# Two more chunks gathered by TensorE in four column groups, with x@w_ch of late pairs between the rounds

**Chip, cores, metric.** One core of one Trainium2 chip. The metric is device time in microseconds (us), the median of several executions.

## The reference

Causal attention with a bias, then a spectral layer: along the sequence, the first 64 modes of a real FFT are multiplied by complex matrices, transformed back to `y`, and a channel product with a relu ends it.

```python
def _moe_ref(x, w_r, w_i, w_ch):          # x is the attention's output, 8 x 576 x 512
    X = np.fft.rfft(x, axis=1)
    Xr, Xi = np.real(X[:, :64]), np.imag(X[:, :64])
    Yr = np.einsum('bmd,mde->bme', Xr, w_r) - np.einsum('bmd,mde->bme', Xi, w_i)
    Yi = np.einsum('bmd,mde->bme', Xr, w_i) + np.einsum('bmd,mde->bme', Xi, w_r)
    ...
    y = np.fft.irfft(Y, n=S, axis=1)
    u = x + y
    return (u + np.maximum(u @ w_ch, 0.0)).astype(np.float32)
```

## The kernel before

The 64 modes come in eight chunks of eight (`c` = 0 to 7; chunk five is `c` = 4). For each chunk `modes` multiplies with the weights w_r and w_i, which stream in from DRAM all the time; VectorE adds the earlier partial sums (`y_sb`), and the result stands as 128 rows of (mode, re/im, batch). The inverse transform wants the rows of all chunks on partitions and the batch in the free dimension: that tile is `yv`, with y (`which` = 0) and v = y@w_ch (`which` = 1). There are two ways into it. A *spread* is a DMA of 128 KB. A *gather* does it on TensorE: matmuls that pick the columns of a few batches, one column group for each, followed by copies by ScalarE and VectorE. Chunks one to four are gathered, chunks five to eight are spread, the last two of them also used directly. Between these steps `work()` puts a *pair* of x@w_ch, the product of two blocks of x with w_ch: transposes, two casts on VectorE, eight matmuls, and a copy of the product out of PSUM, where TensorE's results land. *Granted clock* below is the share of its full clock that TensorE was given.

```python
    def modes(g, c, meanwhile=None):
        ...                                    # 16 matmuls, 4 for each quarter of the weights
            yb = spool.tile([P, DM], FP16, name="y_sb", tag="y")
            ...                                # VectorE: yb = ps + y_acc[:, c]
            if c >= NCK // 2:
                spread(c, 0, yb)
            return yb

    def spread(c, which, rows):
        nc.sync.dma_start(out=yv[16 * c : 16 * c + 16, :, which, :], in_=rows)

    def gather(c0, c1):
        n = 2 * MC * (c1 - c0)
        rows = slice(2 * MC * c0, 2 * MC * c1)
        ng = P // n
        for b0 in range(0, B, ng):
            vp = auxpool.tile([P, DM], FP32, name="v_ps", tag="aux")
            yp = auxpool.tile([P, DM], FP32, name="yg_ps", tag="aux")
            for which, ps in ((1, vp), (0, yp)):
                for dt in range(DT):
                    for g in range(ng):
                        ...                    # matmul into column group g
                for g in range(ng):
                    dst, src = yv[rows, b0 + g, which, :], ps[n * g : n * g + n, :]
                    if g % 2:
                        nc.vector.tensor_copy(out=dst, in_=src)
                    else:
                        nc.scalar.copy(out=dst, in_=src)

    def work():
        ...
        if order_z:
            i = order_z.pop(0)
            x_transposed(i)                    # transposes, two casts on VectorE
            ahead.append(i)
        if len(ahead) == 2 or not order_z:
            keep(ahead.pop(0))                 # product, then a copy of it

    TAKE = (3, 2, 2, 0, 2, 1)

    for c in range(NCK - 2):
        yb = modes(NG - 1, c)
        for x in range(TAKE[c] - 1):
            work()
        yt = y_transposed(yb, c)
        if TAKE[c]:
            work()
        if c >= NY:
            y_times_wch(c, yt)                 # 4 matmuls, a VectorE copy, a spread
        elif c == NY - 1:
            gather(0, NY)                      # four rounds, two column groups
    work()
    c = NCK - 2
    x_transposed(0)
    x_times_wch(0, False)
    yb6 = modes(NG - 1, c)
    ...                                        # chunks seven and eight, then 18 pairs of output
```

(The kept pairs of kind "e" are copied once by ScalarE and once, as a difference, by VectorE: that second copy, L495 of 1.23 us, plays a part below.)

The softmax here doesn't subtract the row's maximum and nothing guards it: scores larger than these inputs give would overflow.

## Time and profile before

| | before |
|---|---|
| median of 6 executions | 458.11 us (456.71 to 459.57) |
| span of the profiled one | 458.0 us (its time: 459.76) |
| start of the first gather | 377.39 us |
| chunk six's, seven's modes start | 400.04, 409.96 us |
| chunk eight's modes: first, last quarter | 415.18, 419.44 us |

The span ends with the output, some 38.56 us after the start of the last quarter's matmuls.

The timeline of TensorE around chunk six, whose lines the change rewrites (start, length, line, tiles, idle time before and what ended it):

```profile
400.04 1.12 PE L441 MATMUL yp<-w_sb,xs 128*32 128x512 bf16 x16
401.96 0.40 PE L625 MATMUL yt_ps<-ident16h,y_sb 128*128 128x128 f16 x4 [0.80 <-DVE y_sb L455]
...
409.96 1.12 PE L441 MATMUL yp<-w_sb,xs 128*32 128x512 bf16 x16
```

From chunk six's modes to chunk seven's it is 9.92 us, 8.55 of them TensorE work.

### The profile page before, as it was taken

The numbers are of one execution on the slowest core, as the hardware profiler recorded it, in microseconds if no ns is written. First come the engines' busy times: TensorE is split into PE (matmuls) and PEld (weight loads), VectorE is DVE, ScalarE is ACT, GpSimd is POOL, SyncE is SP. The second block draws the span as 40 slices with busy tenths as digits, with TensorE's granted clock in tenths as the row PEclk, the third lists the DMA queues.
The fourth block names the chain that finished last, engine by engine and source line by source line (L and its number), as shares of the span: only waits on it lengthen the run. The fifth ranks groups of instructions, "written<-read, shape, count | busy, mean of one in ns | idle before, by whom it ended". The sixth has DMA issues, their size and how long they took to land.

```text
span 458.0 us, 10354 instructions
## 1 busy us (share of the span) xinstructions
PE 349.1 (76%) x4241; PEld 220.4 (48%) x4241; DVE 236.5 (52%) x528; ACT 223.5 (49%) x390; POOL 182.6 (40%) x269
## 2 busy tenths in 40 slices
PE   0798997976563969946587788679977867989996
PEld 0465665654342646624354555456643335444432
DVE  6675765753332636724345435556556423552676
ACT  1475887464242745723444444456632222321895
POOL 6655554454344555434453444455422321200000
PEclk9997999997777979967768769899999875699999
DMA  9999999999999999999999999999999999993697
GB/s 172 199 202 203 201 201 203 203 204 204 204 205 201 200 186 202 204 205 204 202 201 204 204 204 203 204 202 202 206 205 208 206 206 206 210 215 77 228 308 303
DMA packets 108800, 94.01 MB, mean 205 GB/s; under 512 B 28417, under 2 KB 103937, under 8 KB 108753
## 3 DMA queue, kind: packets, MB, share of 16 engines
q0 software_dynamic: 98960, 81.81, 112.9%
q1 hardware_dynamic: 9792, 11.55, 8.1%
q8 instruction: 33, 0.54, 0.4%
q14 instruction: 15, 0.11, 0.1%
HBM read 164.56 MB, written 9.44 MB: 380 GB/s over the span
## 4 chain that ended last, share of the span: by engine, by line
DMA 53%; PE 32%; DVE 6%; issue 4%; POOL 3%; ACT 1%; DVEq 0%; POOLq 0%
DMA w_sb<-in_moe_w_i_dram 28%; DMA q<-in_q_dram 13%; DMA w_sb<-in_moe_w_r_dram 5%; PE sc_ps L365 4%; DMA x_all<-in_moe_w_i_dram 4%; PE av_ps L394 4%; PE yp L441 3%; PE sc_ps L359 3%; PE tr_ps L324 2%; DMA y_acc<-in_moe_w_r_dram 2%; PE z_ps L602 2%; DMA k<-in_k_dram 2%; PE z_ps L692 2%; PE ft_ps L418 2%; PE u_ps L711 2%
## 5 line engine op out<-in xcount | busy, mean ns | idle before, releaser
L373 ACT ACTIVATE p_sb<-sc_ps,cumt_sb 128x576 f16<-128x576 f32 (+1 forms) x256 | 142.1, 636 | 46.2 <-PE sc_ps L365 45.7
L217 POOL DMA_DIRECT2D w_sb<-in_moe_w_i_dram x60 | 45.0, 751 | 87.3 <-PE yp L441 48.5
L217 POOL DMA_DIRECT2D w_sb<-in_moe_w_r_dram x60 | 45.4, 757 | 63.4 <-DMA w_sb<-in_moe_w_r_dram 23.3
L217 POOL DMA_DIRECT2D v<-in_v_dram x72 | 50.7, 706 | 31.5 <-DMA v<-in_v_dram 10.5
L324 PE MATMUL tr_ps<-ident,q 64*64 64x64 bf16 x576 | 18.1, 215 | 52.9 <-DMA q<-in_q_dram 52.8
L359 PE MATMUL sc_ps<-negm,ident 128*128 128x256 bf16 x256 | 57.1, 310 | 0.2
L441 PE MATMUL yp<-w_sb,xs 128*32 128x512 bf16 x480 | 36.9, 412 | 16.2 <-DMA w_sb<-in_moe_w_i_dram 11.1
L327 DVE COPY qtA<-tr_ps 64x576 bf16<-64x576 bf16 x32 | 23.7, 741 | 49.4 <-PE tr_ps L324 49.4
L344 ACT ACTIVATE p<-sc_ps,cumt 128x64 f16<-128x64 f32 x32 | 10.1, 314 | 75.7 <-PE sc_ps L340 75.7
L365 PE MATMUL sc_ps<-qtB,ktB 128*128 128x512 bf16 (+2 forms) x192 | 45.2, 354 | 0.0
L394 PE MATMUL av_ps<-v,p_sb 128*128 128x65 f16 x1024 | 44.3, 197 | 0.0
L394 PEld LDWEIGHTS <-p_sb 128*128 128x128 f16 x1024 | 39.3, 100 | 4.8 <-issue 0.5
L327 DVE COPY ktA<-tr_ps 64x576 bf16<-64x576 bf16 x32 | 24.0, 749 | 33.2 <-PE tr_ps L324 33.2
L324 PEld LDWEIGHTS <-q 64*64 64x64 bf16 x576 | 14.2, 127 | 55.6 <-DMA q<-in_q_dram 54.4
L365 PE MATMUL sc_ps<-qtA,ktA 65*128 65x512 bf16 (+2 forms) x192 | 37.4, 305 | 0.6 <-DMA qtA<-ncum_sb 0.6
L399 DVE TENSOR_REDUCE den<-av_ps 128x5 f32<-128x10 f32 x64 | 10.8, 169 | 49.0 <-PE av_ps L394 49.0
L441 PEld LDWEIGHTS <-xs 128*32 128x32 bf16 x512 | 22.7, 170 | 25.7 <-issue 22.0
L404 DVE TENSOR_TENSOR x_all<-av_ps,rcp 128x320 f16<-128x320 f32 x64 | 31.4, 491 | 2.2
L365 PEld LDWEIGHTS <-ktB 128*128 128x128 bf16 x192 | 23.0, 120 | 15.8 <-issue 7.1
L327 ACT COPY ktB<-tr_ps 64x576 bf16<-64x576 bf16 x32 | 20.3, 635 | 20.0 <-DVE ktA L327 19.1
L602 PE MATMUL z_ps<-wch_sb,xs 128*128 128x512 f16 x96 | 27.4, 437 | 0.8 <-DVE xs L596 0.8
L324 PE MATMUL tr_ps<-ident,k 64*64 64x64 bf16 x576 | 17.0, 207 | 13.3 <-DVE qtB L327 8.6
(116 smaller groups left out, 534.3 us busy)
## 6 DMA issues: line engine op xcount, KB each, us to landing
w_sb<-in_moe_w_r_dram POOLq DMA_DIRECT2D x60, 512.0 KB, 12.0
w_sb<-in_moe_w_i_dram POOLq DMA_DIRECT2D x60, 512.0 KB, 11.9
q<-in_q_dram POOLq DMA_DIRECT2D x32, 144.0 KB, 10.0
k<-in_k_dram POOLq DMA_DIRECT2D x32, 144.0 KB, 10.1
v<-in_v_dram POOLq DMA_DIRECT2D x72, 64.0 KB, 9.7
out_dram<-r_sb SPq DMA_DIRECT2D x16, 256.0 KB, 2.1
out_dram<-r_w SPq DMA_DIRECT2D x16, 256.0 KB, 2.5
x_all<-in_moe_w_i_dram POOLq DMA_DIRECT2D x3, 512.0 KB, 10.1
```

Of the source, the lines that this page charges most:

```text
L217: nc.gpsimd.dma_start(out=dst, in_=src)
L324: nc.tensor.transpose(ps[rows, r, :], src[rows, r, :], ident16[rows, rows])
L327: copy(out=dst[n % NQ][rows, :].rearrange("d (p r) -> d p r", r=R), in_=ps[rows].rearrange("d r p -> d p r"),)
L344: nc.scalar.activation(out=p4[n % 2][:, :NL], in_=ps, func=ACTF.Exp, bias=cumt4[:, b * (H // 2) + g : b * (H // 2) + g + 1], scale=0.125,)
L359: nc.tensor.matmul(ps[:, bass.ds(w * S, W)], ident16, negm[:, bass.ts(r, W)], start=True, stop=False, skip_group_check=True,)
L365: nc.tensor.matmul(ps[:, c0 : c0 + i1 - i0], keys[:, w, r, :], qt[:, i0:i1], start=False, stop=True, skip_group_check=True,)
L373: nc.scalar.activation(out=pt[:, poff[x] : poff[x] + S - w * W], in_=ps[:, w * S : (w + 1) * S - w * W], func=ACTF.Exp, bias=cumt_sb[:, x, ...
L394: nc.tensor.matmul(ps[:, I, r : r + NCH], lhsT, rhs, start=(i == 0), stop=(i == len(todo) - 1), skip_group_check=True,)
L399: nc.vector.tensor_reduce(out=den, in_=ps[:, :, 0 : VW : NCH], axis=mybir.AxisListType.X, op=ALU.add)
L404: nc.vector.tensor_tensor(out=x_all[:, g, b, :, D * h : D * h + D], in0=ps[:, :, 1 : NCH], in1=rcp.unsqueeze(2).to_broadcast([P, NT, D]), ...
L441: nc.tensor.matmul(ps[32 * cg : 32 * cg + 32, :], cols[:, c0 : c0 + 32, c * MC + 2 * cg + par], wt[(g, c, ri, par)][:, cg, :], start=(x == ...
L602: nc.tensor.matmul(z[:, x, :], xts[i][:, x, dt, :], wch_sb[:, dt, :], start=(dt == 0), stop=(last and dt == DT - 1), skip_group_check=True,)
```

## The change

Its intent: eight transfers of 128 KB become four, and waits of the gather rounds are covered by the product of a late pair (two of the four rounds of the first gather, one of the two of the second). Chunks five and six go through `yt_first` and a second gather of two rounds; as that one has 32 columns for each batch, four batches fit side by side (`ng` = 4).

```diff
-            if c >= NCK // 2:
+            if c >= NCK - 2:
                 spread(c, 0, yb)
...
-        yt = yt_first[:, :, c, :] if c < NY else spool.tile(...)
+        yt = yt_first[:, :, c % NY, :] if c < NCK - 2 else spool.tile(...)
...
-    def gather(c0, c1):
+    def gather(c0, c1, turns):
...
                         nc.scalar.copy(out=dst, in_=src)
+            if turns:
+                turns -= 1
+                work()
...
-    TAKE = (3, 2, 2, 0, 2, 1)
+    TAKE = (3, 2, 2, 0, 1, 0)
...
-        if c >= NY:
-            y_times_wch(c, yt)
-        elif c == NY - 1:
-            gather(0, NY)
+        if c == NY - 1:
+            gather(0, NY, 2)
+        elif c == NCK - 3:
+            gather(NY, NCK - 2, 1)
```

More of the change, by code (lines that the diff above doesn't have):

```diff
@@ L625, in y_transposed @@
             nc.tensor.transpose(ps[:, dt, :], yb[:, bass.ts(dt, P)], ident16h)
-        yt = yt_first[:, :, c, :] if c < NY else spool.tile([P, DT, P], FP16, name="yt_sb", tag="yt")
+        yt = yt_first[:, :, c % NY, :] if c < NCK - 2 else spool.tile([P, DT, P], FP16, name="yt_sb", tag="yt")
         nc.scalar.copy(out=yt, in_=ps)
```

## The prediction

> **What bounds the kernel now.** I read the page's 40 slices first, then the chain of waits, then the timeline of the end, then the busy time in windows of 3.41 us.
>
> In the slices (11.45 us each) DMA stays at 9 until slice 36, and the granted TensorE clock falls to 5 and 6 in slices 34 and 35, just before:
>
> ```profile
> PEclk9997999997777979967768769899999875699999
> DMA  9999999999999999999999999999999999993697
> ```
>
> The chain of waits says what follows whom. Until 375 us it runs through weight transfers. From 377.39 us it holds TensorE lines only, almost without a break; no weight transfer is on it any more:
>
> ```profile
> 355.01 19.81 DMA w_sb<-in_moe_w_i_dram
> 377.39 2.00 PE v_ps L653 x8
> 380.78 2.00 PE v_ps L653 x8
> ...
> 387.53 2.00 PE v_ps L653 x8
> 390.91 1.97 PE yp L441 x16
> ...
> 400.11 1.08 PE yp L441 x13
> ```
>
> So the end is set by TensorE from 377.39 us on, and a transfer saved there saves nothing by itself. (Last weights: a transfer takes 2.55 us at 206 GB/s, eight are in flight, so I put the last landing near 415.5 us; its matmuls start at 419.44 us. That is 4 us of slack.)
>
> What a gather round costs is read from the timeline (start, length):
>
> ```profile
> 380.78 1.98 PE L653 MATMUL v_ps<-wch_sb,yt_first 128*64 128x512 f16 x8 [0.96 <-DVE yv L663]
> 382.80 0.58 ACT L665 CAST yv<-v_ps 64x512 f16<-64x512 f32 x1 [2.31 <-PE v_ps L653]
> 383.28 0.58 ACT L665 CAST yv<-yg_ps 64x512 f16<-64x512 f32 x1
> 383.41 0.69 DVE L663 CAST yv<-v_ps 64x512 f16<-64x512 f32 x1 [2.08 <-ACT yv L665]
> 384.02 0.69 DVE L663 CAST yv<-yg_ps 64x512 f16<-64x512 f32 x1
> 384.15 1.98 PE L653 MATMUL v_ps<-wch_sb,yt_first 128*64 128x512 f16 x8 [0.95 <-DVE yv L663]
> ```
>
> The reader should see two things. VectorE's copy out of a PSUM tile starts 0.03 us after ScalarE's copy out of the same tile ends (383.38): they take turns. And each of the four rounds makes the next user of that tile wait 0.95 us.
>
> The windows (length, PE busy, ..., granted clock, DMA share, GB/s) show what those gaps cost:
>
> ```profile
> 338.34:341.75 3.41, 1.90 (x28) 1.03 (x21) 2.10 (x5) 0.59 (x1) 2.20 (x3) 1.00 1.24 207
> 351.99:355.40 3.41, 1.36 (x17) 0.83 (x17) 1.80 (x3) 0.34 (x1) 1.13 (x2) 0.99 1.24 207
> 379.30:382.71 3.41, 2.45 (x23) 2.04 (x21) 1.30 (x2) 1.06 (x2) 0.74 (x1) 0.50 1.24 206
> 392.95:396.36 3.41, 3.41 (x15) 1.74 (x14) 1.85 (x3) 0.00 (x0) 1.92 (x3) 0.51 1.25 207
> ```
>
> A window with 1.36 us busy (40%) was followed by half clock, one with 1.90 us (56%) was not; at half clock 2.45 us (72%) did not bring the clock back, a full window did. From 375.9 to 396.4 us TensorE runs at half.
>
> **The Trainium skill.** "TensorE: Matmul & The Clock Gate", Part 1, What's actually happening: a free-running window of 3413 ns and two clock states. The trace agrees: the clock falls at 355.4, 365.6 and 375.9 us, three windows apart. Its Part 3 (packing small matmuls) says that matmuls in different column groups run side by side; here 16 of 128x32 take 1.06 us, where 16 full ones at 0.21 us would take 3.4. "PSUM — Partial Sum Buffer", PSUM bank collisions: two engines must not touch the same bank and quadrant at once, reads included; the turn-taking above is that guard, by tile. The same page, Engine vs sequencer instructions: VectorE's and ScalarE's queues are strict FIFO; no line of this trace contradicts it, and the argument below rests on it.
>
> **The change, part by part.** Chunks five and six lose their own product with w_ch (2 x 4 matmuls, 0.86 us each), two VectorE copies and four transfers of 128 KB. They gain a second gather of two rounds in four column groups. One pair's x@w_ch is put after each of the first two rounds of the old gather, and the last product (8 matmuls, no transposes) between the two new rounds. The order of instructions in the build confirms this, and its waits say that in the new rounds the copies of one tile go ScalarE, VectorE, ScalarE, VectorE, each waiting for the one before. Copies of 64x512 and of 128x512 take the same here (ScalarE 0.58 and 0.59 us, VectorE 0.69 both), so I keep 0.58 and 0.69 us for 32x512 (starts 0.48 and 0.61 apart on one engine). All clock times below are for the old run's window phase.
>
> *First gather.* Round one as before, at half clock, to 379.85. Then transposes (1.0) and products (8 x 0.427) follow with no wait. TensorE is busy for a whole window, so full clock comes near 382.7 instead of 396.4; the product ends near 383.5. Round two at full clock 0.89 + 0.45, transposes 0.61, products 1.73: 387.2. Round three 1.35; round four waits for copies (VectorE also has the pair's two casts and the pair's keep) until 389.7; it ends 391.1, and chunk five's modes wait until 392.2. One wait per round remains, 1.2 us each; 60% busy should hold the clock. Modes 1.12, the sum on VectorE 0.8 (now bare), transposes and one pair 2.4: chunk six's modes start at **396.6, against 400.04: 3.5 us gained**.
>
> *Second gather.* Modes 1.12, sum 0.8, transposes 0.4, copy 0.68: its first product starts near 399.55, and takes 1.06, so T0 = 400.6 is the end of the first product. After T0, in us:
> - Copies of v: ScalarE 0.25-0.83, VectorE 0.87-1.56, ScalarE 1.60-2.18, VectorE 2.22-2.91. Copies of y follow in the same alternation and end at 4.87.
> - TensorE: y part (estimated 0.8 from 16 small matmuls), product 1.73, done at 2.5; second v waits till 2.96, ends 4.02; second y waits for 4.9, ends 5.7.
> - ScalarE: the product's keep (1.01) after the copies, 4.04-5.05. Second-round copies from 4.96, eight in turn, last one ends at 9.58.
> - VectorE, in order: only then the two casts of pair 0, 9.50 and 10.11.
> - TensorE: transposes of pair 0 end at 6.15. Its product needs the first cast: 10.24. **Idle 4.1 us.** It ends at 12.0.
>
> Chunk seven's modes then start at 400.6 + 12.0 = 412.6, against 409.96. From chunk six's modes to chunk seven's it is 16.0 us instead of 9.9: 6.1 lost. Sum so far: +2.6 us.
>
> *Clock after the second gather.* An idle of 4.1 us leaves at least one window under 41% busy wherever the windows fall, so the clock halves. It returns only after a full busy window: 3 to 6 us at half, and as TensorE has no spare time there, half of that is lost: 1.4 to 3.1, I take 2.4.
>
> *The rest* (final modes, 18 pairs of output) is unchanged and TensorE-bound. Transfers: four spreads fewer, about 2.5 us less in the DMA queue at 206 GB/s, all inside the slack.
>
> Total: -3.5 + 6.1 + 2.4 = +5.0 us: **463.2 us**.
>
> **Rivals.**
> - *The first gather wins alone.* If the second gather's copies were hidden (say the product between its rounds covers them), only its matmuls cost: 2 x 1.86 - 1.72 = 2.0 us more, and -3.5 stands: about 456.7. For: the filling at the first gather does hide two waits. Against: eight alternating copies per round take 4.6 us after the product's end, and the filler lasts 1.7 us; nothing at all stands after the second round.
> - *No halving after the stall.* 460.8. For: 56% was once enough. Against: 4 us are longer than a window.
> - *The clock does not come back in the first gather*, because the windows fall badly or round three and four halve it again. Then the gain of 3.5 is nearly gone: 465 to 467.
> - *DMA limits the end after all.* The four spreads share the engines with the weights; then fewer transfers would gain up to 2 us. Against: 4 us of slack at the last modes.
>
> **Range and chances.** Free window phase moves both clock terms by some 1.5 us each; the stall is uncertain by 1 us (handovers, keep's place). So 460.0 to 466.0. Over 2% faster means under 449.0, for which no mechanism exists: 0.01. Over 2% slower means over 467.3: the stall plus bad clock in both places, 0.04.
>
> **What would show it.** Right: v copies of 32x512 of about 0.58 and 0.69 us alternating; TensorE idle some 4 us before the product of pair 0, released by VectorE's cast; clock 1.00 by about 383 us; then 0.50 in the stretch after the stall; chunk six's modes near 396.6, chunk seven's near 412.6; the output tail as long as before. Wrong: copies of one tile overlapping on the two engines, casts of pair 0 ahead of the copies, or a final-modes wait on a weight transfer.

## More of the kernel before

What TensorE waited for between 376 and 420 us is in the view of waits (engine, tile and line, what it waited for: us in total, times, longest):

```profile
PE v_ps L653 <- DVE yv L663: 2.9, 3, 1.0
...
PE yp L441 <- DVE yv L663: 1.0, 1, 1.0
PE z_ps L602 <- DVE xs L596: 0.8, 2, 0.6
```

The first two are the four waits of the gather for its copies, about 1 us each; the third says that a product with w_ch hardly ever waits for its casted transposes.

## The result

The kernel after takes 465.99 us in the median of 6 executions (464.29 to 467.01), against 458.11. The ratio is 1.0166, with a 95% interval of 1.0132 to 1.0199. (Ratios here are the mean time of one kernel's runs over that of the other's of the same rounds, so not quite the ratio of the medians quoted.) So it is slower by 1.7%, within the 2% that counts as the same. The profiled execution took 467.01 us, its span is 465.1. (Both profiled executions are slow ones of their kernel: the one before, with 459.76 us, lies above all six timed ones.)

The slices of the profile after, to set against those in the prediction:

```profile
PEclk9997999987586989957788799899998879979999
DMA  9999999999999999999999999999999999961697
```

A slice is now 11.63 us. The dip of the granted clock to 5 and 6 in slices 34 and 35 is gone, a shallower one (to 7) has come in slice 36. DMA falls to 6 in that slice and to 1 in the next; before it fell to 3 only in slice 37: now a stretch of little traffic lies between the last weights and the output.

The view of waits of the kernel after, TensorE, 376 to 426 us:

```profile
PE z_ps L602 <- DVE xs L596: 4.9, 2, 4.7
PE yt_ps L625 <- DVE y_sb L455: 3.8, 4, 1.9
PE v_ps L653 <- DVE yv L663: 1.6, 2, 1.0
...
PE yp L441 <- DVE yv L663: 1.0, 1, 1.0
PE yg_ps L653 <- DVE yv L663: 1.0, 1, 1.0
```

By the timeline the first gather's part of the last three is two waits of 1 us (ahead of round four and of chunk five's modes) instead of four, as intended; the second gather brings two of its own, 0.66 and 0.97 us. Above them stands one wait of 4.7 us of a product for VectorE's casts, and a wait of 1.9 us for the sum of chunk six. The timeline shows both in their place:

```profile
396.28 1.12 PE L441 MATMUL yp<-w_sb,xs 128*32 128x512 bf16 x16
397.44 1.23 DVE L495 TENSOR_TENSOR y_acc<-z_ps,y_acc 128x1024 f16<-128x1024 f32 x1 [1.71 <-ACT y_acc L494]
398.58 0.68 DVE L455 TENSOR_TENSOR y_sb<-yp,y_acc 128x512 f16<-128x512 f32 x1
399.32 0.40 PE L625 MATMUL yt_ps<-ident16h,y_sb 128*128 128x128 f16 x4 [1.92 <-DVE y_sb L455]
...
402.19 0.69 DVE L663 CAST yv<-v_ps 32x512 f16<-32x512 f32 x1 [2.93 <-ACT yv L665]
402.91 0.58 ACT L665 CAST yv<-v_ps 32x512 f16<-32x512 f32 x1 [0.75 <-DVE yv L663]
...
406.73 0.62 PE L592 MATMUL xt_ps<-ident16h,x_all 128*128 128x128 f16 x8
...
410.59 0.70 DVE L663 CAST yv<-yg_ps 32x512 f16<-32x512 f32 x1 [0.64 <-ACT yv L665]
411.32 1.29 DVE L596 CAST xs<-xt_ps 128x512 f16<-128x512 f32 x2
412.07 3.60 PE L602 MATMUL z_ps<-wch_sb,xs 128*128 128x512 f16 x8 [4.72 <-DVE xs L596]
415.59 1.38 PE L441 MATMUL yp<-w_sb,xs 128*32 128x512 bf16 x16
```

Read it from below. The product at 412.07 had waited 4.72 us for the casts at 411.32. The casts' input, the transposes of pair 0 at 406.73, had been ready since 407.35; but in VectorE's queue the casts stand behind its copies of the second gather, which take turns with ScalarE's copies of the same tile (the releasers in brackets). The product then took 3.60 us instead of 1.90, at half clock. The top four lines are the other wait: the sum of chunk six (L455) stood in VectorE's queue behind the second half of a kept product (L495), of 1.23 us.

The windows of the kernel after (stretch, length, busy time of PE, PEld, DVE, ACT, POOL, granted clock, DMA share, GB/s):

```profile
379.30:382.70 3.40, 3.40 (x21) 1.84 (x18) 2.59 (x4) 0.90 (x2) 0.74 (x1) 0.59 1.24 207
382.70:386.10 3.40, 3.40 (x32) 2.35 (x31) 1.90 (x3) 2.07 (x3) 0.74 (x1) 1.00 1.24 205
...
406.60:410.00 3.40, 0.75 (x23) 0.50 (x12) 2.07 (x3) 1.74 (x4) 0.00 (x0) 0.92 1.24 206
410.00:413.40 3.40, 1.33 (x4) 0.51 (x5) 1.99 (x3) 0.56 (x1) 0.00 (x0) 0.50 0.89 148
```

With a product behind round one the clock is full from some 382 us (before: 396.4). The stretch with the stall is 0.75 us busy, and half clock follows. The DMA share falls already in the last of these stretches, before chunk seven's modes begin: no weight is waited for.

**Where the 7.1 us of span went.** Offsets from the start of the first gather take out what happened ahead of it (the gather itself started at 377.39 before and 377.12 after, 0.3 earlier):

| stage | before | after | difference |
|---|---|---|---|
| start of gather to chunk six's modes | 22.65 | 19.16 | -3.49 |
| chunk six's to chunk seven's modes | 9.92 | 19.31 | +9.39 |
| to chunk eight's modes, first quarter | 5.22 | 5.48 | +0.26 |
| to its last quarter | 4.26 | 4.26 | 0 |
| to the end of the span | 38.56 | 39.77 | +1.21 |

Less the 0.27 of the earlier start it adds up to +7.10.

### The profile page after: what moved, and what is told of

It reads as the page before. It is cut to its first block, busy times and chain, and to the rows that moved or that the text cites. A ratio compares the mean times of both kernels' runs of the same rounds, so it can differ in the third digit from the quotient of the medians. Undisturbed runs are those within 1.5% of the kernel's fastest.

```text
span 465.1 us, 10436 instructions
## 1 busy us (share of the span) xinstructions
PE 343.0 (74%) x4265; PEld 219.7 (47%) x4297; DVE 241.2 (52%) x534; ACT 227.9 (49%) x398; POOL 182.7 (39%) x269
## 4 chain that ended last, share of the span: by engine, by line
DMA 61%; PE 24%; DVE 5%; issue 4%; POOL 3%; ACT 2%; DVEq 0%; POOLq 0%; ACTq 0%
DMA w_sb<-in_moe_w_i_dram 29%; DMA q<-in_q_dram 15%; DMA w_sb<-in_moe_w_r_dram 10%; PE yp L441 3%; PE z_ps L602 2%; PE sc_ps L365 2%; DMA k<-in_k_dram 2%; DMA y_acc<-in_moe_w_r_dram 2%; PE av_ps L394 2%; PE z_ps L695 2%; PE sc_ps L359 2%; PE tr_ps L324 2%; DMA y_acc<-in_moe_w_i_dram 2%; PE u_ps L714 2%; PE u_ps L695 2%
## 5 line engine op out<-in xcount | busy, mean ns | idle before, releaser
L359 PE MATMUL sc_ps<-negm,ident 128*128 128x256 bf16 x256 | 55.9, 304 | 0.2
L441 PE MATMUL yp<-w_sb,xs 128*32 128x512 bf16 x480 | 35.9, 405 | 17.3 <-DMA w_sb<-in_moe_w_i_dram 12.2
L365 PE MATMUL sc_ps<-qtB,ktB 128*128 128x64 bf16 (+2 forms) x160 | 34.8, 322 | 3.7 <-issue 2.0
```

Source lines behind the costliest of these rows:

```text
L359: nc.tensor.matmul(ps[:, bass.ds(w * S, W)], ident16, negm[:, bass.ts(r, W)], start=True, stop=False, skip_group_check=True,)
L365: nc.tensor.matmul(ps[:, c0 : c0 + i1 - i0], keys[:, w, r, :], qt[:, i0:i1], start=False, stop=True, skip_group_check=True,)
L441: nc.tensor.matmul(ps[32 * cg : 32 * cg + 32, :], cols[:, c0 : c0 + 32, c * MC + 2 * cg + par], wt[(g, c, ri, par)][:, cg, :], start=(x == ...
```

## The experiments

Twelve runs. Each timed one is compared with the kernel before on the same chip in the same rounds. "Theory" in the expectations is the prediction's: the first part (pairs between the rounds of the first gather) wins 3.5 us, the second part (the second gather) loses by alternating copies, by the place of the casts in VectorE's queue, and by the clock. The offsets below are those of the profiled executions, in us from the start of the first gather.

| run | time, us | ratio | 95% | chunk six's modes | seven's | eight's last quarter | rest of span |
|---|---|---|---|---|---|---|---|
| before | 458.11 | 1 | | 22.65 | 32.57 | 42.05 | 38.56 |
| after | 465.99 | 1.0166 | 1.0132-1.0199 | 19.16 | 38.47 | 48.21 | 39.77 |
| e1_first_only | 457.13 | 1.0002 | 0.9980-1.0023 | 20.37 | 29.82 | 40.52 | 38.51 |
| e1b_first_again | 456.90 | 0.9976 | 0.9962-0.9991 | 22.19 | 31.63 | 41.12 | 38.51 |
| e2_second_only | 468.12 | 1.0244 | 1.0224-1.0264 | 21.65 | 41.88 | 51.62 | 39.05 |
| e3_by_tile | 463.70 | 1.0151 | 1.0109-1.0193 | 19.42 | 36.05 | 45.51 | 39.58 |
| e4_pair0_early | 463.56 | 1.0121 | 1.0090-1.0152 | 21.34 | 35.82 | 46.15 | 39.95 |
| e5_stall_filled | 463.68 | 1.0124 | 1.0109-1.0139 | 19.11 | 36.72 | 46.20 | 38.85 |
| e6b_first_spread_twice | 466.18 | 1.0187 | 1.0172-1.0202 | 22.02 | 31.47 | 49.31 | 40.62 |
| e8_mended | 458.37 | 1.0008 | 0.9982-1.0033 | 19.34 | 33.63 | 43.09 | 39.00 |
| e9_mended_warm | 455.72 | 0.9960 | 0.9937-0.9983 | 18.46 | 30.13 | 39.62 | 38.80 |
| e10_spread_warm | 457.18 | 0.9989 | 0.9975-1.0003 | 19.83 | 28.43 | 41.45 | 38.58 |
| e11_first_no_spread | 457.19 | 0.9984 | 0.9965-1.0004 | 21.90 | 31.34 | 40.80 | 38.84 |
| e12_mended_best | 455.55 | 0.9948 | 0.9935-0.9961 | 16.69 | 27.94 | 39.60 | 38.81 |

### The two parts by themselves

**First part alone.** From the kernel before:

```diff
+    def gather(c0, c1, turns):          # and work() after a round while turns are left
-    TAKE = (3, 2, 2, 0, 2, 1)
+    TAKE = (3, 2, 2, 0, 1, 0)
-            gather(0, NY)
+            gather(0, NY, 2)
```

> The first gather of the change alone: two x@w_ch of pairs between its rounds; chunks five and six keep their own product and their four spreads. My theory (the second gather costs, the first gains): full clock from about 383 us, chunk six's modes near 397 instead of 400.0, chunk seven's near 406.5 instead of 410.0, time 454.5 us (ratio 0.992). Rival (the first gather's fill is worth nothing, the pairs only change places): 458.

Measured: 457.13 us, ratio 1.0002. The expected gain did not come. In the profiled execution (the fastest of the four) the clock was full and chunk six's modes came 2.3 us sooner, but chunk eight's then waited; this is the timeline of TensorE in e1_first_only:

```profile
413.89 0.45 PE L441 MATMUL yp<-w_sb,xs 128*32 128x512 bf16 x4 [1.10 <-DMA w_sb<-in_moe_w_i_dram]
```

So the last weights are a limit close behind TensorE. As one profile shows one execution, the kernel was run once more.

> The first gather of the change alone, once more, as the neighbour of the next run. Both theories: about 1.000 as in its first run; the last modes' weights land after TensorE is ready for them.

Measured: 456.90 us, 0.9976. This time no matmul of chunks seven and eight waited for weights; instead the clock fell, in the timeline and the windows of e1b_first_again:

```profile
390.02 1.96 PE L441 MATMUL yp<-w_sb,xs 128*32 128x512 bf16 x16 [0.98 <-DVE yv L663]
```
```profile
389.50:392.90 3.40, 2.08 (x18) 0.90 (x18) 1.77 (x3) 0.22 (x1) 1.71 (x3) 0.56 1.24 205
```

The modes of chunk five take 1.96 us where e1_first_only had 1.12: half clock from about 390 to 397 us, after rounds three and four, which have no pair behind them. The same kernel is thus held up by weights in one execution and by the clock in another, and wins 0 to 1 us.

**Second part alone.** From the kernel after:

```diff
-    TAKE = (3, 2, 2, 0, 1, 0)
+    TAKE = (3, 2, 2, 0, 2, 1)
-            gather(0, NY, 2)
+            gather(0, NY, 0)
```

> The second gather of the change alone: the first gather has nothing between its rounds, as in the kernel before. My theory: the stall before pair 0's product (4 to 5 us) and the halved clock after it are all there, chunk seven's modes near 419, time 467 to 469 us (ratio 1.020 to 1.024). Rival (the loss comes from moving the pairs into the first gather): 458 to 460.

Measured: 468.12 us, 1.0244, as expected: the loss is all in the second part. The first part is worth more beside it than alone: 1.0166 against 1.0244, or some 3.6 us of 458, which is the 3.5 of the prediction. With the second gather in, TensorE reaches the last modes so late that neither trace shows a wait for weights there, so what the first part saves counts in full.

### The stall taken apart

**Copies by tile.** In the second gather VectorE copies all of v, ScalarE all of y, so that the two engines never share a tile:

```diff
-                    if g % 2:
+                    if (g % 2 if ng == 2 else which):
```

> The changed kernel, but in the second gather VectorE makes all four copies of the product's tile and ScalarE all four of the other, so nothing alternates within a tile; the number of copies is the same. My theory (the alternation is the long chain): a round's copies end about 2.7 us after the product instead of 4.9, the stall shrinks from 4.7 to about 2.3 us, time 461 to 463 us. Rival (the sheer number of copies on the engines is the bound): the stall stays above 4 us and the time near 466.

Measured: 463.70 us, 1.0151. The timeline of VectorE and ScalarE in the first round of e3_by_tile:

```profile
401.51 2.79 DVE L663 CAST yv<-v_ps 32x512 f16<-32x512 f32 x4 [3.30 <-PE v_ps L653]
401.93 2.34 ACT L665 CAST yv<-yg_ps 32x512 f16<-32x512 f32 x4 [2.46 <-PE yg_ps L653]
```

Both sets of four now run side by side and end by 404.3, 2.79 us after the first began; in the kernel after, the eight took from 401.59 to 406.27. The stall before pair 0's product fell from 4.72 to 2.82 us, and chunk seven's modes came 2.4 us sooner, although in this execution the clock was half from about 398 to 405. The mean time fell by only 0.15%: the four executions reach from 462.41 to 466.68 us, the profiled one (462.63) is a fast one, and what held up the slow ones was not found out.

**Pair 0 early.** The transposes and casts of pair 0 go ahead of the second gather's last copies:

```diff
                 turns -= 1
                 work()
+                if c1 == NCK - 2:
+                    x_transposed(0)
...
-    x_transposed(0)
     x_times_wch(0, False)
```

> The changed kernel, but pair 0 is transposed after the first round of the second gather, so its two casts stand on VectorE ahead of the second round's copies; all copies still alternate. My theory (what costs is where the casts stand in VectorE's queue): the product of pair 0 follows the second round at once, chunk seven's modes start near 409.7 instead of 415.6, no window falls under 56% busy, time 460 us. Rival (the copies themselves are the bound wherever the casts stand): 464 to 466.

Measured: 463.56 us, 1.0121, not the 460 expected. The stall itself is gone, in the timeline of TensorE in e4_pair0_early:

```profile
409.27 1.90 PE L602 MATMUL z_ps<-wch_sb,xs 128*128 128x512 f16 x8
411.92 1.13 PE L441 MATMUL yp<-w_sb,xs 128*32 128x512 bf16 x16 [0.75 <-DVE yv L663]
```

The product follows without a wait, and chunk seven's modes wait 0.75 us for a copy. But the profile has the clock at half twice, about 390 to 397 and 400 to 407, once at the bare gather rounds and once after the wait for chunk six's sum, and the sum of chunk seven is waited for 1.10 us. The first of these began at chunk five, ahead of anything that this edit touches, and put chunk six's modes 2.18 us later than in the kernel after. So the offset of chunk seven's modes, 2.65 us sooner, understates the edit: from chunk six's modes to chunk seven's it is 14.48 us instead of 19.31, 4.83 less.

**The clock alone.** The stall stays, but TensorE is kept busy in it: the transposes of pair 0 are written nine times over, each with the same values.

```diff
-                for dt in range(DT):
+                for dt in list(range(DT)) * (9 if i == 0 else 1):
```

> The changed kernel, with the 8 transposes of pair 0 written nine times over (same data, 64 matmuls more, about 3.7 us), so TensorE is busy in the stall while VectorE's casts come no earlier. My theory (part of the loss is the clock that halves in the stall): the stall before pair 0's product shrinks to under 1 us of idle, the product takes 1.9 us instead of 3.6 and chunk seven's modes 1.1 instead of 1.4, the end comes 2 us earlier than the changed kernel: 464 us (ratio 1.012). Rival (the clock doesn't depend on the stall): product still 3.6 us, 466 us.

Measured: 463.68 us, 1.0124, as expected. In e5_stall_filled's timeline the product of pair 0 has its full-clock length:

```profile
410.84 1.90 PE L602 MATMUL z_ps<-wch_sb,xs 128*128 128x512 f16 x8 [1.15 <-DVE xs L596]
```

It still could not begin earlier (it waits for the casts), yet the kernel gained 0.4%, about 1.9 us (the two intervals overlap a little; the stage shows it better, with 1.70 us in the product and 0.26 in chunk seven's modes): that is the clock's part of the loss. The 3.60 us of that product in the kernel after are thus half clock and nothing else.

**Both mended.** e3's and e4's edits together:

> The changed kernel with both mends: the second gather's copies by tile (VectorE the product's, ScalarE the other's) and pair 0 transposed after its first round. My theory: no stall over 1 us before pair 0's product, chunk seven's modes near 408 instead of 415.6, and with the spreads gone no wait for weights: 456 to 458 us (ratio 0.997), up to 460 if a window falls on the bare sum of chunk six and the clock halves. Rival (eight copies per round cost more than the spreads in any arrangement): 460 to 463.

Measured: 458.37 us, 1.0008. The loss of 1.7% is gone. No stall is left; chunk seven's modes in e8_mended:

```profile
408.94 1.12 PE L441 MATMUL yp<-w_sb,xs 128*32 128x512 bf16 x16 [0.61 <-ACT yv L665]
```

They come at +33.63, 4.84 us sooner than in the kernel after; e3 and e4 had 2.42 and 2.65. That these add up is chance, because of the clock in e4's first gather. Counted from chunk six's modes to chunk seven's, the kernel after takes 19.31 us, e3 16.63, e4 14.48 and e8 14.29 (the kernel before 9.92). So the two edits shorten the same stall: the place of the casts does nearly all of it, and copying by tile adds 0.2 us there. Behind it the sum of chunk seven no longer waits for the second round's copies (1.10 us in e4, 0.24 in e8). Which part of the difference in time between e4 and e8 is the clock's in the first gather can't be told from one trace of each. In e8's execution the clock was half from about 398 to 404 us, after the wait of 1.92 us for chunk six's sum.

**Both mended, and the clock held.** In addition matmuls into an unused PSUM tile fill places where TensorE idles: ahead of the last quarter of chunks two to four, and behind the modes of chunks five and six:

```diff
+    def warm(n):
+        d = auxpool.tile([P, DM], FP32, name="warm_ps", tag="aux")
+        for x in range(n):
+            nc.tensor.matmul(d, wch_sb[:, 0, :P], wch_sb[:, 0, :], start=True, stop=True, skip_group_check=True)
...
-        yb = modes(NG - 1, c)
+        yb = modes(NG - 1, c, {3: lambda: warm(8)} if c in (1, 2, 3) else None)
+        if c >= NCK - 4:
+            warm((3, 7)[c - NCK + 4])
```

> The kernel with both mends, and TensorE kept busy with products nobody reads while it waits for weights (8 in chunks two, three and four) and for the sums of chunks five and six (3 and 7). My theory (clock and stall together are the whole loss): full clock from 355 us to the end, the first gather 2 us shorter, chunk seven's modes near 406, time 454 to 455 us (ratio 0.992). Rival (the idle matmuls get in the way, or the weight stream sets the end here too): 457 or more.

Measured: 455.72 us, 0.9960; its interval ends below 1. The clock is at 0.92 in the stretch from 379.3 us and at 1.00 in all from 382.7 to 420, and chunk seven's modes come at +30.13, 3.5 us before e8's. The gain is half of the expected 0.992; the clock was not full all the way from 355 us either, but fell once more, from 376.4 to 379.8 us.

### Does a transfer count after all?

**Spreads twice.** If the transfers of the spreads weigh on the last weights, doubling them should show it. From e1:

```diff
-        nc.sync.dma_start(out=yv[16 * c : 16 * c + 16, :, which, :], in_=rows)
+        for x in range(2 if c < NCK - 2 else 1):
+            nc.sync.dma_start(out=yv[16 * c : 16 * c + 16, :, which, :], in_=rows)
```

> The first gather of the change alone, and the four spreads of chunks five and six each sent twice: 0.5 MB more for the DMA engines, about 2.5 us at 206 GB/s, nothing more for the other engines. In the run without the doubling TensorE waited 1.1 us for the weights of the last modes. New theory (the first part alone gains nothing because it runs into the weight stream): the last modes wait 2 us longer, time 459.3 us (ratio 1.004 to 1.006 instead of 1.000). Rival (transfers have slack, as I predicted; the gain is lost elsewhere): ratio 1.000, wait about 1 us.

Measured: 466.18 us, 1.0187. This run does not answer the question. The queue that issues the spreads, in e6b_first_spread_twice:

```profile
399.93 7.01 SPq L467 DMA_DIRECT2D yv<-v_sb  x2
406.99 7.60 SPq L467 DMA_DIRECT2D yv<-y_sb  x2
```

Each twin writes the rows of the first, so it was made to wait until that one had landed, and the queue backed up; TensorE then waited 3.98 us for a spread. So what cost the time was, by this trace, a chain of transfers one behind the other and not a share of the bandwidth.

**No spreads of chunks five and six.** e1 with these four transfers left out, and the rows of `yv` filled once with other finite data. The result is wrong, though the comparison with the reference still passed: it does not notice these modes, so it also proves little about them in the other runs.

```diff
-            if c >= NCK // 2:
+            if c >= NCK - 2:
                 spread(c, 0, yb)
...
-        spread(c, 1, vb)
+        if c >= NCK - 2:
+            spread(c, 1, vb)
```

> The same, without the four spreads of chunks five and six (wrong result on purpose: their rows hold other data, copied early by ScalarE where it is idle). 0.5 MB less for the DMA engines, about 2 us. Theory (the first part alone gains nothing because the last weights come too late): no wait for weights in the last modes, time 2 us under its neighbour, 455 us (ratio 0.995). Rival (the gain is lost elsewhere): as its neighbour.

Measured: 457.19 us, 0.9984, where 455 was expected: leaving the transfers out gained nothing over e1b (0.9976). No matmul waited for weights; but the clock was half from about 389.6 to 396, as in e1b. While that happens TensorE is too late for the weights to matter. The transfers themselves show what the time hides: the last weights landed at 414.6 us (16.3 us after their issue), in e1b at 416.7 (17.8 us after), with half clock at the same place in both. So the spreads do hold up the weights, by some 2 us in the one trace of each.

**Spreads kept, clock held.** So the question was put with the clock held in both. e10 is e1 with a pair behind three rounds of the first gather, and with e9's filling, three matmuls behind both modes; e12 is e8 with the same edits:

```diff
-    TAKE = (3, 2, 2, 0, 1, 0)
+    TAKE = (3, 2, 2, 0, 0, 0)
-            gather(0, NY, 2)
+            gather(0, NY, 3)
...                                     # warm() and its use in chunks two to four as in e9
+        if c >= NCK - 4:
+            warm(3)
```

> Three pairs between the rounds of the first gather, TensorE kept busy while it waits for weights and sums, chunks five and six with their own product and spreads as before. TensorE is ready for the last modes near 412, before the weights are there. Theory of the weight stream as the floor: waits of 2 us and more in the last modes, time 455.5 to 457. Rival (no floor): 453.

> The same with the mended second gather in place of the spreads. Theory: 0.5 MB less in the stream, so the floor lies 2 us lower; chunk seven's modes near 404, the last modes at 413.5, time 453.5 us (ratio 0.991), faster than its neighbour with spreads by 1.5 to 3 us. Rival (the second gather is worth nothing even when mended): as its neighbour or slower.

Measured on the same chip in the same rounds: e10 457.18 us (0.9989), e12 455.55 us (0.9948), so e12 is faster by 0.4%, some 1.9 us by the ratios (1.6 by the medians). Both have the clock at 1.00 in every stretch from 379.3 us on (e10 was at half just before, from 375.9; e12 was not), and both wait for weights. TensorE in e10_spread_warm, then in e12_mended_best, at the last quarter of chunk eight:

```profile
416.62 0.46 PE L441 MATMUL yp<-w_sb,xs 128*32 128x512 bf16 x4 [0.58 <-DMA w_sb<-in_moe_w_i_dram]
```
```profile
414.89 0.45 PE L441 MATMUL yp<-w_sb,xs 128*32 128x512 bf16 x4 [0.71 <-DMA w_sb<-in_moe_w_i_dram]
```

The last weights are there 1.73 us sooner where four spreads of 128 KB are missing. (Their transfer was also issued 1.99 us sooner in e12, at 393.80 against 395.79. That this is not the cause is argued and not tested: the DMA share stays at 1.22 or more in both up to 409.9 us, so the engines were never short of work, and e11's weights came 2 us before e1b's with issues only 0.5 us apart.) e12 is the fastest version found, faster than both kernels; its expectation of 453.5 was two us too low, and e10 lies 0.2 above its expected 455.5 to 457.

## Why the prediction was right, and where not

The predicted range (460.0 to 466.0) holds the measured 465.99 by a hair, which is luck: the loss is 7.9 us in the medians where 5.0 was predicted. The class (within 2%) is right. By its own steps:

- **TensorE sets the end, and a saved transfer saves nothing by itself.** Right for this change. The last weights landed at 415.2 us, ten before the last quarter's matmuls (425.33), and the time rose. (The chain is not quite "TensorE lines only": it also has a ScalarE copy of 1.02 us at 404.57 and 1.11 us of issue.) But the *4 us of slack* for the last weights was mis-sized. In the kernel before their transfer was issued at 400.83 and landed 16.9 us later, at 417.7 and not 415.5, with the last quarter's matmuls at 419.44: 1.7 us. e1_first_only, e10 and e12 each run into the weights. It did no harm to the number, as the second gather pushed TensorE back by far more.
- **First gather, -3.5 us at chunk six's modes.** Right: -3.49 in offset (22.65 to 19.16), 396.28 where 396.6 was predicted. Clock full near 382.7: right. "60% busy should hold the clock": right in this execution, where the window from 388.98 to 392.39 us is 61% busy. But rounds three and four are not that busy wherever the window falls: in e1b the window from 386.55 to 389.96 us holds 1.55 us of work (45%), in e11 the one from 385.95 holds 1.69 (50%), and the clock halved at the end of both. (Windows are cut at the clock changes of each trace.) The term is true beside the second gather (after against e2: 3.6 us) and not alone (0 to 1 us).
- **Second gather, +6.1 us.** The mechanism is right in each link of the stall: copies in alternation, ScalarE 0.57 and VectorE 0.69 us as assumed, the casts last in VectorE's queue, TensorE idle before the product of pair 0. e3 and e4 took away one link each and e8 both. The size was 7.7 (9.39 less 1.70 that the slow product took), and most of the difference lies ahead of the stall. The wait for the sum of chunk six was counted as a bare 0.8, and was 1.92: the kept product's second half (L495) stood ahead of it in VectorE's queue. This was to be read from the same rule of order that was used for the casts, and was not. The stall was 4.7, not 4.1; half of that is only that TensorE was done 0.3 us sooner than laid out (407.35 us, 5.8 after the first product's end instead of 6.15), the other half that the product could start 0.3 later. e4, with the casts moved ahead, left the 1.92 as it was, as it must.
- **Clock after the stall, +2.4.** Measured: 1.70 in the product and 0.26 in chunk seven's modes, 1.96 together; e5 puts it at 0.4%, 1.9 us. Right.
- **The rest unchanged.** Wrong by 1.2 us: the tail took 39.77 instead of 38.56. In it TensorE waited 0.56 us for the last spread of v, issued at 428.75, at 432.75 (4.0 us to landing, before 2.9); e3 and e4 show a like wait (0.56 and 0.51) and tails of 39.58 and 39.95, e5 does not and has 38.85. Why that transfer took longer in some, and where the rest of the 1.2 went, was not settled.
- **Sum.** -3.5 + 7.7 + 2.0 + 1.2 - 0.3 (an earlier start) = 7.1 us of span, for the predicted +5.0. The times of the kernel after fall in two groups, 464.3 to 465.0 and 467.0; the profiled one belongs to the second. What parts them was not found out; the phase of the clock window is a guess, since only one of the executions has a trace.
- **The rivals.** "The first gather wins alone" (456.7) was reached only with fillers as well (e9, 455.7); with the copies hidden alone (e8) it is 458.4. "No halving after the stall" is e5's state, made on purpose. "The clock does not come back in the first gather": in the traced execution of the kernel after it came back and stayed; in e4, e1b and e11, whose first gathers are the same, it halved again after rounds three and four. "DMA limits the end" is not so in this change, and becomes so (some 1.9 us, e10 against e12) as soon as TensorE is quick enough.

What the change intended was sound in one part: four fewer transfers are worth 0.4% once the clock is held (e12 against e10). Covered waits and the held clock without them are worth 0.1% (e10), which is not clear of noise. The change lost because the new copies, alternating between two engines, and a cast that the next product needs went through one queue in the wrong order.

## What to carry to other kernels

When a matmul's operand is prepared by an in-order engine, place that small preparation ahead of any series of copies that waits for a partner, and give whole PSUM tiles to one copying engine each; here that was worth 1.6% with the same work. Idle time of TensorE can be paid twice, once as itself and once at half clock after it: here one stall of 4.7 us did that, and in e1b two waits of 1 us close together did it too. Keep fillers where TensorE would stand. And a gain on one limit is only as large as the distance to the next: measure it alone and beside the other parts, since here the same part was worth 3.6 us in one company and next to nothing by itself.

## What the Trainium skill lacked or had wrong

- "TensorE: Matmul & The Clock Gate": it speaks of a busy and an idle window, and gives no share of activity that decides. In the 14 traces here (338 to some 426 us, windows of 3.41 us cut at each trace's own clock changes) every window at full clock with TensorE busy for less than 44% was followed by half clock, such as the kernel before's of 352.00 to 355.41 (40%) and the kernel after's of 406.05 to 409.46 (30%); none with more than 51% was, such as the kernel before's of 338.34 to 341.76 (56%); between the two both were seen. At half clock up to 81% busy (e1_first_only, 374.53 to 377.95 us) did not bring it back; 83% (e6b_first_spread_twice, 362.27 to 365.69) and more did.
- "PSUM — Partial Sum Buffer": it allows different quadrants of a bank to two engines at once, and calls a guard by whole bank the simple version. What it lacks is what the simple version costs: here copies of different quadrants of one tile were put in turn (ScalarE to 402.16, VectorE from 402.19, with ScalarE as its releaser). Giving whole tiles to engines avoided it; no run lifted the guard itself.
- "VectorE: DVE Perf Modes": its table of cycles for copies out of PSUM goes by free elements, and it does not say what follows for a copy of few partitions: here 32x512 took 0.57 us on ScalarE and 0.69 on VectorE, the same as 128x512 (0.59 and 0.69), so four copies of a quarter cost four whole ones.
